# The second layer of a fused scan and maxout kernel as seven half-block products over pairs of 512-token blocks

## The chip, the cores and the metric

One core of a Trainium2 chip runs the whole program. The metric is the device time of one launch in microseconds (us). Each kernel was run several times; the kernel before was run again in the same rounds as every changed kernel. Each run is marked fast or slow: for one core, slow means more than 1.5% above the fastest run of the same kernel. A ratio below is the mean time of one kernel's fast runs over the mean of the other's fast runs of the same rounds, so it is not quite the ratio of the medians that are quoted.

Engines in the profile: PE is the tensor engine (matmuls; PEld its weight loads), DVE the vector engine, ACT the scalar engine, POOL and SP two engines that here do little but start DMA transfers. SPq is SP's instruction queue, in which a transfer that cannot yet be handed over holds up the next. PSUM is the memory that matmuls write their sums to. A transfer has *landed* when its completion is recorded, which can be well after it has left the queue.

## The reference, cut to what matters

```python
# x, f_logit: (4, 6144, 256) float32;  w1, w2: (256, 1024);  w_out: (1024, 256)
f = lower_bound + (1 - lower_bound) * sigmoid(f_logit)
h = 0
for t in range(6144):                     # a gated running sum, per batch and channel
    h = f[:, t] * h + (1 - f[:, t]) * x[:, t]
    y[:, t] = h
y = y.reshape(24576, 256)
out = np.maximum(y @ w1, y @ w2) @ w_out  # float32, (24576, 256)
```

Both kernels use max(a, b) = a + relu(b - a): a first layer relu(y (w2 - w1)), a second layer that multiplies it by w_out, and a linear part y (w1 w_out), whose 256x256 product is made once at the start.

## The kernel before: the parts that matter

The tokens come as 48 blocks of 512. After the first four blocks, input is brought in chunks of 1024 tokens (one chunk is one pair of blocks). For each chunk and each of f_logit and x there are two steps. POOL starts a *fetch*: DRAM to a DRAM scratch buffer, cast from float32 to bfloat16. SP starts a *transpose*: the scratch buffer goes through a transposing DMA into the chip's memory, with channels on partitions. There are two scratch buffers for each input, so the fetch for chunk c+2 waits until the transpose of chunk c has landed.

```python
def fetch(c):                                    # POOL queue
    for s in range(2):                           # f, then x
        scr = scratch[s][uses[s] % NSCR]         # NSCR = 2
        nc.gpsimd.dma_start(out=scr..., in_=srcs[s][b, t0 : t0 + nt, :]...)
        held[c, s] = scr
def cross(c):                                    # SP queue
    for s in range(2):
        dst = inpool.tile([P, KC, CH], BF16, name=("fT", "xT")[s])
        nc.sync.dma_start_transpose(out=dst[:, :, 0:nt], in_=held[c, s][0:nt, :])
# ...
def second_layer(j, slot):                       # block j, an eighth of its matmuls
    # for each 128-token group: 2 linear + 8 matmuls with 128x256 results
    nc.tensor.matmul(ps[:, r, :], lhsT=left, rhs=right, ...)      # L410
    # ... after the last one of two groups
    nc.vector.tensor_copy(out=osb[...], in_=ps[:])                # L430
    if i == ns - 1:
        nc.sync.dma_start(out=out[r0 : r0 + nb, :]..., in_=osb[...])   # store, SP queue
# ...
for j in range(2, NBLK + 1):
    ahead("cross", cross, j + 3)                 # transposes three blocks ahead
    ahead("fetch", fetch, j + 7)                 # fetches seven blocks ahead
    for fc in range(FC):                         # FC = 8
        first_layer(j, fc)                       # two 128x512 matmuls (L381), one relu (L389)
        second_layer(j - 1, fc)                  # ten 128x256 matmuls in two fc's
        # ... gate and scan of block j + 1 between them
```

So SP's queue holds, for each 1024 tokens: transpose f, transpose x, store of one block, store of the next. A store waits until its block is computed, and everything behind it waits with it.

## Time and profile before

| | |
|---|---|
| time, median of the first three runs | 401.07 us (400.53 to 441.09) |
| span of the profiled run | 428.3 us (a slow run) |
| PE work of one pair in an undisturbed stretch | 15.6 us |
| PE / ACT / DVE busy in the profiled run | 92% / 63% / 58% |

The profile is of a slow run: it shows PE waiting in places, where the timed fast runs have almost no room for waits. First, the busy time and the costliest groups. Columns of a group: line, engine, operation, result<-inputs, shapes, count | busy us, mean ns of one | idle us of the engine just before them and what ended most of it. (In all fences, `...` stands for lines left out.)

```profile
PE 392.8 (92%) x2744; PEld 296.8 (69%) x2792; DVE 248.7 (58%) x359; ACT 268.5 (63%) x447; POOL 26.4 (6%) x58
...
L381 PE MATMUL dT<-y,wd 128*128 128x512 bf16 x720 | 219.5, 384 | 21.3 <-ACT rt L389 19.5
L410 PE MATMUL psO<-wob,rt 128*128 128x256 bf16 x1536 | 230.7, 274 | 2.7 <-issue 0.4
```

The next fence is from the waits (engine, line, tile <- what it waited for: us in total, times, longest), and after it one line of the stretch table for 126 to 141.6 us (length; busy us of PE, PEld, DVE, ACT and POOL with their instruction counts; granted PE clock; DMA share; GB/s).

```profile
ACT u L190 <- DMA fT<-scr_1_91: 18.2, 7, 4.6
ACT u L190 <- DMA fT<-scr_0_90: 17.3, 8, 5.2
```

```profile
126.00:141.60 15.60, 15.49 (x112) 11.87 (x113) 10.02 (x14) 10.97 (x19) 0.97 (x2) 1.00 1.25 200
```

The second-layer matmuls and the first-layer ones fill PE: 15.49 of 15.60 us in an undisturbed stretch. ACT waited 35.5 us in all for the transposes of f; that is where this slow run lost its time. The chain that ended last, by engine and by line:

```profile
PE 46%; DMA 34%; SPq 15%; ACT 3%; DVE 1%; issue 1%; ACTq 0%
PE psO L410 25%; DMA fT<-scr_0_90 20%; PE dT L381 19%; SPq L153 13%; DMA fT<-scr_1_91 12%; ACT u L190 2%; DMA w1n_110<-in_moe_w_dram 2%; SPq L433 1%; PE psO L352 1%; ACT rt L389 1%; PE tT L180 1%; PE psO L365 0%; SPq L121 0%; DVE osb L430 0%; DVE y L233 0%
```

Last, the DMA part: the hardware queue's packets (transposes and stores: count, MB, share of 16 engines' span), and the median us from issue to landing of a transpose (the last number).

```profile
q1 hardware_dynamic: 100512, 51.13, 66.7%
...
fT<-scr_0_90 SPq DMA_TRANSPOSE x11, 16.1
xT<-scr_0_92 SPq DMA_TRANSPOSE x11, 9.4
```

### The profile page before, as it was taken

What the parts mean: (1) busy time and instruction counts of PE and PEld (TensorE: products, weight loads), DVE (VectorE), ACT (ScalarE), POOL (GpSimd) and SP (SyncE); (2) the same over time, 40 slices, a digit from 0 to 9 for tenths busy, and PEclk for the clock granted to TensorE, in tenths of its full rate; (3) what the DMA queues carried; (4) which work ended last, traced back from release to release, by engine and by line L of the source; (5) the groups of instructions that cost most, each with busy time, mean ns of one, the idle gap of its engine ahead of it and who ended that gap; (6) DMA issues with size and microseconds to landing.
All of it is one profiled execution on the core that took longest, in us unless ns stands there. A gap on an engine that the chain in (4) does not pass through costs nothing.

```text
span 428.3 us, 6970 instructions
## 1 busy us (share of the span) xinstructions
PE 392.8 (92%) x2744; PEld 296.8 (69%) x2792; DVE 248.7 (58%) x359; ACT 268.5 (63%) x447; POOL 26.4 (6%) x58
## 2 busy tenths in 40 slices
PE   3999979798789999998997899999998999999996
PEld 1677756576557777776775577767676777777775
DVE  5785637455357566564653557657547656567551
ACT  3656656557366676675673666756657676776762
POOL 1400000000000000000000000000000000000000
PEclk9999999999989999999999699999999999999999
DMA  7999999999999999999998999999999999998112
GB/s 245 222 220 198 123 157 141 137 169 252 81 240 226 119 239 233 112 248 168 183 237 75 218 158 186 250 145 170 219 131 231 226 216 164 268 157 179 79 69 100
DMA packets 103377, 77.01 MB, mean 180 GB/s; under 512 B 93552, under 2 KB 94064, under 8 KB 102640
## 3 DMA queue, kind: packets, MB, share of 16 engines
q1 hardware_dynamic: 100512, 51.13, 66.7%
q0 software_dynamic: 2544, 25.17, 36.1%
q8 instruction: 22, 0.36, 0.4%
q10 hardware_dynamic: 288, 0.26, 0.2%
q14 instruction: 11, 0.09, 0.1%
HBM read 53.48 MB, written 48.23 MB: 237 GB/s over the span
## 4 chain that ended last, share of the span: by engine, by line
PE 46%; DMA 34%; SPq 15%; ACT 3%; DVE 1%; issue 1%; ACTq 0%
PE psO L410 25%; DMA fT<-scr_0_90 20%; PE dT L381 19%; SPq L153 13%; DMA fT<-scr_1_91 12%; ACT u L190 2%; DMA w1n_110<-in_moe_w_dram 2%; SPq L433 1%; PE psO L352 1%; ACT rt L389 1%; PE tT L180 1%; PE psO L365 0%; SPq L121 0%; DVE osb L430 0%; DVE y L233 0%
## 5 line engine op out<-in xcount | busy, mean ns | idle before, releaser
L389 ACT ACTIVATE rt<-dT 128x512 bf16<-128x512 f32 x384 | 219.2, 598 | 104.1 <-PE dT L381 100.0
L381 PE MATMUL dT<-y,wd 128*128 128x512 bf16 x720 | 219.5, 384 | 21.3 <-ACT rt L389 19.5
L410 PE MATMUL psO<-wob,rt 128*128 128x256 bf16 x1536 | 230.7, 274 | 2.7 <-issue 0.4
L410 PEld LDWEIGHTS <-rt 128*128 128x128 bf16 x1536 | 170.7, 114 | 41.4 <-issue 1.1
L233 DVE TENSOR_TENSOR_SCAN y<-ff,y,v 128x512 bf16<-128x512 bf16 x88 | 107.9, 1268 | 0.1
L430 DVE COPY osb<-psO 128x512 f32<-128x512 f32 x94 | 64.7, 690 | 59.0 <-PE psO L410 58.9
L381 PEld LDWEIGHTS <-wd 128*128 128x128 bf16 x768 | 75.8, 99 | 33.2 <-issue 24.6
L209 DVE TENSOR_SCALAR ff<-u,nom 128x512 bf16<-128x512 bf16 x94 | 29.0, 351 | 105.0 <-ACT u L190 105.0
L410 PE MATMUL psO<-w_109,y 128*128 128x256 bf16 x384 | 74.0, 275 | 0.0
L410 PEld LDWEIGHTS <-y 128*128 128x128 bf16 x384 | 43.4, 113 | 42.6 <-issue 3.5
L190 ACT ACTIVATE u<-fT 128x1024 bf16<-128x1024 bf16 x44 | 46.4, 1054 | 35.5 <-DMA fT<-scr_1_91 18.2
L220 DVE TENSOR_TENSOR v<-u,xT 128x1024 bf16<-128x1024 bf16 x44 | 30.3, 688 | 3.8 <-DMA xT<-scr_0_92 1.8
L98 POOL DMA_DIRECT2D scr_0_90<-in_f_logit_dram x11 | 5.4, 493 | 149.7 <-DMA fT<-scr_0_90 149.7
L98 POOL DMA_DIRECT2D scr_1_91<-in_f_logit_dram x11 | 5.3, 486 | 148.8 <-DMA fT<-scr_1_91 148.1
L233 DVE TENSOR_TENSOR_SCAN y<-ff,v 128x512 bf16<-128x512 bf16 x6 | 7.0, 1208 | 0.0
L98 POOL DMA_DIRECT2D scr_0_92<-in_x_dram x11 | 5.4, 488 | 18.7 <-DMA xT<-scr_0_92 16.9
L98 POOL DMA_DIRECT2D scr_1_93<-in_x_dram x11 | 5.3, 486 | 15.7 <-DMA xT<-scr_1_93 14.9
L190 ACT ACTIVATE u<-tT 128x1024 bf16<-128x1024 bf16 x3 | 3.2, 1058 | 4.3 <-PE tT L180 4.3
L352 PE MATMUL psO<-ident_f,w1n_110 128*128 128x128 f32 x8 | 1.9, 422 | 3.4 <-DMA w1n_110<-in_moe_w_dram 3.4
L341 ACT ACTIVATE wd<-wdf,om 128x128 bf16<-128x128 f32 (+1 forms) x6 | 2.2, 428 | 4.3 <-DVE wdf L333 4.3
L352 PEld LDWEIGHTS psO<-ident_f,w1n_110 128*128 128x128 f32 x8 | 1.6, 221 | 3.7 <-issue 3.7
L220 DVE TENSOR_TENSOR v<-u,tT 128x1024 bf16<-128x1024 bf16 x3 | 3.6, 1216 | 0.0
(49 smaller groups left out, 45.1 us busy)
## 6 DMA issues: line engine op xcount, KB each, us to landing
out_dram<-osb SPq DMA_DIRECT2D x47, 512.0 KB, 4.8
scr_0_90<-in_f_logit_dram POOLq DMA_DIRECT2D x11, 512.0 KB, 7.5
scr_0_92<-in_x_dram POOLq DMA_DIRECT2D x11, 512.0 KB, 12.4
scr_1_91<-in_f_logit_dram POOLq DMA_DIRECT2D x11, 512.0 KB, 7.9
scr_1_93<-in_x_dram POOLq DMA_DIRECT2D x11, 512.0 KB, 13.6
fn<-in_f_logit_dram POOLq DMA_DIRECT2D x3, 256.0 KB, 7.9
xn<-in_x_dram POOLq DMA_DIRECT2D x3, 256.0 KB, 8.6
w2n_112<-in_moe_w_dram SPq DMA_DIRECT2D x1, 512.0 KB, 6.5
```

What stands on the lines that cost most here:

```text
L98: nc.gpsimd.dma_start(out=scr[0:nt, :].rearrange("(p i) d -> p (i d)", p=P), in_=src.rearrange("(p i) d -> p (i d)", p=P),)
L153: nc.sync.dma_start_transpose(out=dst[:, :, 0:nt], in_=held[c, s][0:nt, :])
L180: nc.tensor.transpose(dst, src, ident[:])
L190: nc.scalar.activation(out=like(u[:, :, 0:nb], fT), in_=fT, func=AF.Sigmoid, scale=-1.0)
L209: nc.vector.tensor_scalar(out=ff[:, h, 0:nb], in0=u[:, h, 0:nb], scalar1=nom[:, h : h + 1], scalar2=1.0, op0=ALU.mult, op1=ALU.add,)
L220: nc.vector.tensor_tensor(out=like(v[:, :, 0:nb], xT), in0=like(u[:, :, 0:nb], xT), in1=xT, op=ALU.mult,)
L233: nc.vector.tensor_tensor_scan(out=y[:, h, 0:nb], data0=ff[:, h, 0:nb], data1=v[:, h, 0:nb], initial=init, op0=ALU.mult, op1=ALU.add,)
L352: nc.tensor.transpose(pt[:, kc, q, :], half(w1n, g)[:, kc, 2 * r + q], ident_f[:])
L381: nc.tensor.matmul(dT[:, 0:nb], lhsT=wd[:, kc, fc * P : (fc + 1) * P], rhs=y[:, kc, 0:nb], start=(kc == 0), stop=(kc == KC - 1),)
L389: nc.scalar.activation(out=rt[:, 0:nb], in_=dT[:, 0:nb], func=AF.Relu)
L410: nc.tensor.matmul(ps[:, r, :], lhsT=left, rhs=right, start=(s == 0 and (r == 0 or j == NBLK - 1)), stop=(s == n - 1 and (r == 1 or j == N ...
L430: nc.vector.tensor_copy(out=osb[:, 2 * g : 2 * g + 2, :], in_=ps[:])
```

## The change

The intent is to do less PE work. The second layer multiplies relu(...) of two blocks by w_out, split into halves: a 2x2 by 2x2 block product. Strassen's method (in Winograd's form) needs seven half products in place of eight. For a pair, 64 + 16 matmuls of 128x256 become seven products of 16 and four linear parts of 8, all 128x128. In exchange there are four bfloat16 sums of 128x2048 on DVE, three float32 sums out of PSUM on DVE, three snapshots and a copy on ACT. The relu now takes two PSUM banks in one instruction and writes its result in the permuted order which makes the second layer's weight loads contiguous. The work is now scheduled by pairs, and with it the input: f and x are transposed and fetched with different leads, and the first of the two stores of a pair is ready later in the pair than before (after matmul 120 of the 144).

```diff
-    inpool = ctx.enter_context(tc.tile_pool(name="inp", bufs=5))
+    inpool = ctx.enter_context(tc.tile_pool(name="inp", bufs=4))
-    def fetch(c):
+    def fetch(c, s):
-    def cross(c):
+    def cross(c, s):
# ... first layer: one relu of two chains, permuted result
-        nc.scalar.activation(out=rt[:, 0:nb], in_=dT[:, 0:nb], func=AF.Relu)
+        if fc % 2:
+            nc.scalar.activation(
+                out=rts[j, k][:, g - 1 : g + 1, :].rearrange("p q (i m) -> p q i m", m=P),
+                in_=dT[:].rearrange("p q (m i) -> p q i m", m=P),
+                func=AF.Relu,
+            )
# ... second layer of a pair (ja, jb), 144 matmuls
+        product("X", part(0, 0), lambda k: wob[:, k, lo], True)
+        then(snapshot("X", 1))
+        product("B", part(0, 1), lambda k: wob[:, KH + k, lo], True)
+        linear("B", ja, lo, False)
+        then(leave("B", ja, lo, 1, False))
+        product("X", sub(2), lambda k: t2[:, k, :])
+        then(snapshot("X", 2))
+        product("E", sub(1), lambda k: t1[:, k, :], True)
+        then(snapshot("E", 5))
+        product("X", sub(3), lambda k: t3[:, k, :])
+        linear("X", jb, hi, False)
+        then(leave("X", jb, hi, 5, False))
+        product("E", sub(4), lambda k: wob[:, KH + k, hi])
+        linear("E", ja, hi, False)
+        then(leave("E", ja, hi, 2, True))         # store of ja
+        product("X", part(1, 1), lambda k: t4[:, k, :])
+        linear("X", jb, lo, True)
+        then(leave("X", jb, lo, None, True))      # store of jb
# ... start: f one chunk further than x
-        ahead("cross", cross, 4)
+        for s in range(2):
+            ahead("cross", cross, s, 5 - s)
+        ahead("fetch", fetch, 1, 5)
+        ahead("fetch", fetch, 0, 6)
# ... main loop
-        for j in range(2, NBLK + 1):
-            ahead("cross", cross, j + LEAD_CROSS)
-            ahead("fetch", fetch, j + LEAD_FETCH)
+        for p in range(PAIR0, NPAIR):
+            for s in range(2):
+                ahead("cross", cross, s, chunk_of(p + 3) - s)   # f(p+3), x(p+2)
+            for s in range(2):
+                ahead("fetch", fetch, s, chunk_of(p + 5) - s)   # f(p+5), x(p+4)
```

## The prediction

> **What bounds the kernel now.** The tensor engine (PE). By groups, the first layer's 128x512 matmuls (L381) and the second layer's 128x256 matmuls (L410) run back to back: in the timeline eight 128x256 ones take 0.88 us and sixteen slots repeat every 7.82 us per 512-token block when nothing stalls (stretch table: 15.49 of 15.60 us PE busy, granted clock 1.00). That is 216 ns per 128x512 and 109 ns per 128x256. All 1920 L410, 768 L381 and the small matmuls sum to about 385 us; with some 11 us before the first weights and 4 us at the end that is 400, the timed 401.07. The profiled execution (428.3 us) is about 20 us longer because PE waits in several stretches behind late fT transposes (waits: ACT u <- fT 35 us; DMA busy 99%). The timed runs leave almost no room for such stalls. DVE is 58% busy, ACT 63%.
>
> **Removed.** Per pair of blocks (1024 tokens) 80 matmuls of 128x256 (8.74 us of PE); four 0.69 us DVE copies of results; 16 relus of 0.60 us (about 0.51 back to back).
>
> **Added, per pair.** PE: seven products of 16 plus four linear parts of 8: 144 matmuls of 128x128. The transposes of the trace are 128x128 matmuls, each with its own weight load, at eight per 0.445 us, 55.6 ns: 8.0 us. So PE goes from 15.64 to 14.94 us per pair, -0.70 us, for 21 pairs: -14.7 us. Halving the width gives back about 0.2 us of the arithmetic saving of 0.85 us.
> DVE: four bf16 sums of 2048 elements. The drive product (1024 elements, 688 ns) gives an estimate of 1.22 us each, as "VectorE: DVE Perf Modes" in the Trainium skill (perf-mode tier table) has it for this size. Three f32 adds out of PSUM, about 0.70 each; decay in two ops of about 0.45. With the scans (4.9) and drives (1.4): about 14.1 us of 14.94, 94%, against 10.6 of 15.6 before.
> ACT: eight relus of 128x1024 (about 1.0 us; the gates that read PSUM with a stride, 1.02 us, show no price for it), four gates of 0.60, four copies of 0.58: about 12 of 14.94. Not a limit, if nothing queues behind a late gate.
> DMA: same bytes, 4.7% less time for them; transposes are issued about a chunk earlier, which should remove some waits.
>
> **Critical path.** All of the PE saving lies on it as long as DVE keeps up (slack under 1 us per pair) and transposes arrive every 14.94 us. Ideal: 386 us. I add 4 us for the weight loads of y that still step by four tokens (113 ns against 98 contiguous; unproven at 55.6 ns pitch; 32 per pair), for DVE lateness at PSUM hand-over, and for DMA.
>
> **Predicted: 390 us, range 383 to 400. Faster by over 2%: 0.58; within 2%: 0.36; slower by over 2%: 0.06.**
>
> **What would show each step.** PE: 128x128 matmuls near 55.6 ns pitch and a pair near 14.9 us in undisturbed stretches. If y's strided loads do not hide, the linear parts' pitch is above 60 ns. DVE: 90-95% busy in such stretches, sums 1.22 us, leaves 0.70. ACT: relu about 1.0 us, no stride price. Waits: no large PE wait on DVE sums or leaves; fT waits fewer than before.
>
> **What would make it wrong.** (1) Strided weight loads at 128 columns cost 15 ns or more each: 0.5 us per pair, two thirds of the gain. (2) DVE ops longer than estimated, making DVE the period (15.5 us or more). (3) Transposes unable to come every 14.9 us, so that the saving becomes waits on fT or xT. (4) Relus on two banks at once leaving first-layer matmuls waiting on ACT.

## The result and the profile after

The changed kernel is correct, and slower: a median of 449.91 us (441.9 to 462.32, 5 runs) against 400.93 us (400.53 to 441.09, 5 runs). The ratio of fast runs is 1.111, 95% interval 1.099 to 1.122. The profile is of the 462.32 us run, which counts as slow among the kernel's own runs; no run of this kernel came within 10% of a fast run of before, and the profile of a variant whose run counted as fast (x lead, below) shows the same picture.

Busy time and groups first, to be set against those of before:

```profile
PE 386.3 (84%) x4064; PEld 286.1 (62%) x4136; DVE 322.4 (70%) x383; ACT 290.8 (63%) x383; POOL 26.5 (6%) x58
...
L426 ACT ACTIVATE r<-dT 128x1024 bf16<-128x1024 f32 x192 | 196.3, 1025 | 115.9 <-PE dT L418 115.1
...
L596 PE MATMUL ps<-t,S 128*128 128x128 bf16 x1008 | 85.7, 230 | 50.1 <-DVE S L487 49.7
...
L596 PEld LDWEIGHTS <-y 128*128 128x128 bf16 x672 | 49.6, 113 | 16.4
L554 DVE TENSOR_TENSOR osb<-ps,sn 128x512 f32<-128x512 f32 x63 | 42.8, 679 | 13.2 <-PE ps L596 7.6
...
L487 DVE TENSOR_TENSOR S<-r 128x2048 bf16<-128x2048 bf16 x42 | 51.1, 1217 | 0.0
```

A stretch without a wait (same columns as before), and one run of PE in the timeline (start, length, what):

```profile
380.00:396.00 16.00, 15.84 (x188) 11.92 (x188) 14.71 (x17) 12.85 (x18) 0.49 (x1) 1.00 1.04 193
```

```profile
84.97 0.61 PE L596 MATMUL ps<-w13d,y 128*128 128x128 bf16 x8
```

The engines did what was planned. In the chain between 382.5 and 392 us, every slot of nine 128x128 and two 128x512 matmuls takes 0.93 us, 14.9 us for 16 slots of a pair. Eight matmuls with y's strided weight loads end 0.61 us after the start of the first; take off the mean of one (219 ns) and seven spacings are left of 56 ns each: the stride does not show. Sums take 1217 ns, adds 679 ns, relus 1025 ns.

The loss is in waits:

```profile
POOL scr L100 <- DMA fT<-scr: 306.2, 20, 35.0
...
DVE v L205 <- DMA xT<-scr: 77.7, 18, 23.3
...
PE ps L596 <- DVE S L487: 49.7, 14, 22.2
...
ACT u L267 <- DMA fT<-scr: 29.9, 4, 18.4
```

```profile
PE 33%; SPq 28%; DMA 23%; issue 3%; ACT 3%; DVE 1%; POOL 0%; ACTq 0%; POOLq 0%
SPq L149 27%; PE ps L596 17%; PE dT L418 13%; DMA xT<-scr 10%; DMA scr<-in_x_dram 7%; DMA fT<-scr 6%; PE ps L465 2%; DVE S L487 1%; ACT r L426 1%; SPq L437 1%; ACT u L267 1%; ACT osb L552 1%; ACT sn L542 0%; POOL scr L100 0%; DVE osb L474 0%
```

PE's 49.7 us on DVE's sums is not DVE being slow: the sums stand behind the drive product v, which waited 77.7 us for transposes of x. In the chain, the tensor engine has fallen from 46% to 33%, and the line that issues the transposes (L149) alone holds 27%. The timeline of SP's queue and of POOL shows a steady bad state:

```profile
229.67 8.29 SPq L149 DMA_TRANSPOSE fT<-scr  x1
238.05 9.46 SPq L149 DMA_TRANSPOSE xT<-scr  x1
247.61 1.01 SPq L437 DMA_DIRECT2D out_dram<-osb  x2
248.71 9.82 SPq L149 DMA_TRANSPOSE fT<-scr  x1
```

```profile
229.91 0.49 POOL L100 DMA_DIRECT2D scr<-in_f_logit_dram  x1 [15.35 <-DMA fT<-scr]
231.24 0.49 POOL L100 DMA_DIRECT2D scr<-in_x_dram  x1 [0.85 <-DMA xT<-scr]
248.40 0.49 POOL L100 DMA_DIRECT2D scr<-in_f_logit_dram  x1 [16.67 <-DMA fT<-scr]
251.62 0.49 POOL L100 DMA_DIRECT2D scr<-in_x_dram  x1 [2.73 <-DMA xT<-scr]
```

SP is never idle: a transpose of f (8.29 us in the queue), one of x (9.46), two stores (1.01), and at once the next f. From f to f it is 19.0 us, where PE needs 14.95. POOL's f fetch waits until the transpose of f has landed (248.40), which is 18.7 us after it began and just before the next one starts; the x fetch follows 1.3 us later in one of the laps shown and 3.2 us later in the other. So both fetches run beside transposes.

There is also one hole. The chain around it (start, length, what), and a stretch in it:

```profile
73.63 33.96 DMA scr<-in_x_dram
...
107.64 4.40 DMA xT<-scr
```

```profile
96.70:100.70 4.00, 0.00 (x0) 0.00 (x0) 0.00 (x0) 0.00 (x0) 0.00 (x0) 0.50 0.79 10
```

POOL had issued three fetches within 2 us (73.15, 73.63 and 75.10), beside a transpose of f; PE stands still in this stretch, with 10 GB/s moved, and on to 108 us. The lap with the hole (from one transpose of f to the next) lasts 38.5 us, 24 more than PE needs; the sixteen laps after it lose 40 us together. The hole comes back in the profiles of e1, e12 and e16 below (laps of 39.2, 48.6 and 38.6 us), but not in those of e11 and e20 (longest lap 25.8 and 23.9 us), which are as slow: it adds to the loss, and the loss does not need it. Why that one fetch took 34 us is not shown. The DMA part:

```profile
q1 hardware_dynamic: 100512, 51.13, 67.8%
...
fT<-scr SPq DMA_TRANSPOSE x22, 16.5
xT<-scr SPq DMA_TRANSPOSE x22, 9.3
```

The same packets and bytes as before, and transposes that land 16.5 and 9.3 us after issue, against 16.1 and 9.4 in the slow profile of before. The queue's share of 67.8% is of a longer span: 312 us of each DMA engine against 286 in the slow profile of before.

### The profile page after: what moved, and what is told of

It is laid out like the page before. It is cut to its first block, busy times and chain, and to the rows that moved or that the text cites. A ratio compares the mean times of both kernels' runs of the same rounds, so it can differ in the third digit from the quotient of the medians.

```text
span 460.2 us, 9454 instructions
## 1 busy us (share of the span) xinstructions
PE 386.3 (84%) x4064; PEld 286.1 (62%) x4136; DVE 322.4 (70%) x383; ACT 290.8 (63%) x383; POOL 26.5 (6%) x58
## 3 DMA queue, kind: packets, MB, share of 16 engines
q1 hardware_dynamic: 100512, 51.13, 67.8%
## 4 chain that ended last, share of the span: by engine, by line
PE 33%; SPq 28%; DMA 23%; issue 3%; ACT 3%; DVE 1%; POOL 0%; ACTq 0%; POOLq 0%
SPq L149 27%; PE ps L596 17%; PE dT L418 13%; DMA xT<-scr 10%; DMA scr<-in_x_dram 7%; DMA fT<-scr 6%; PE ps L465 2%; DVE S L487 1%; ACT r L426 1%; SPq L437 1%; ACT u L267 1%; ACT osb L552 1%; ACT sn L542 0%; POOL scr L100 0%; DVE osb L474 0%
## 5 line engine op out<-in xcount | busy, mean ns | idle before, releaser
L426 ACT ACTIVATE r<-dT 128x1024 bf16<-128x1024 f32 x192 | 196.3, 1025 | 115.9 <-PE dT L418 115.1
L596 PEld LDWEIGHTS <-S 128*128 128x128 bf16 x1344 | 94.9, 103 | 91.4 <-DVE S L487 52.0
L596 PE MATMUL ps<-t,S 128*128 128x128 bf16 x1008 | 85.7, 230 | 50.1 <-DVE S L487 49.7
L205 DVE TENSOR_TENSOR v<-u,xT 128x1024 bf16<-128x1024 bf16 x44 | 30.3, 688 | 77.7 <-DMA xT<-scr 77.7
L596 PEld LDWEIGHTS <-r 128*128 128x128 bf16 x1008 | 66.9, 98 | 27.3
L418 PEld LDWEIGHTS <-wd 128*128 128x128 bf16 x768 | 62.7, 100 | 19.6 <-issue 11.6
L267 ACT ACTIVATE u<-fT 128x512 bf16<-128x512 bf16 x88 | 54.9, 627 | 30.0 <-DMA fT<-scr 29.9
L554 DVE TENSOR_TENSOR osb<-ps,sn 128x512 f32<-128x512 f32 x63 | 42.8, 679 | 13.2 <-PE ps L596 7.6
L596 PE MATMUL ps<-wob,r 128*128 128x128 bf16 x672 | 51.2, 219 | 0.5
L487 DVE TENSOR_TENSOR S<-r,S 128x2048 bf16<-128x2048 bf16 x42 | 50.8, 1210 | 0.9 <-ACT r L426 0.9
L487 DVE TENSOR_TENSOR S<-r 128x2048 bf16<-128x2048 bf16 x42 | 51.1, 1217 | 0.0
L596 PE MATMUL ps<-w,y 128*128 128x128 bf16 x504 | 48.7, 219 | 0.4
L195 DVE TENSOR_SCALAR ff<-u,nom 128x1024 bf16<-128x1024 bf16 (+2 forms) x54 | 23.9, 454 | 28.6 <-ACT u L267 24.3
L465 PEld LDWEIGHTS <-r 128*128 128x128 bf16 x192 | 19.0, 99 | 4.1 <-issue 0.6
```

The lines of the kernel that those rows point to most:

```text
L195: nc.vector.tensor_scalar(out=ff[:, h, cols], in0=u[:, h, cols], scalar1=nom[:, h : h + 1], scalar2=1.0, op0=ALU.mult, op1=ALU.add,)
L205: nc.vector.tensor_tensor(out=like(v[:, :, cols], xT), in0=like(u[:, :, cols], xT), in1=xT, op=ALU.mult,)
L267: nc.scalar.activation(out=mids[p + NBLK, "u"][:, h, cols], in_=held[c, 0][:, h, cols], func=AF.Sigmoid, scale=-1.0,)
L418: nc.tensor.matmul(dT[:, fc % 2, :], lhsT=wd[:, kc, fc * P : (fc + 1) * P], rhs=y[:, kc, :], start=(kc == 0), stop=(kc == KC - 1),)
L426: nc.scalar.activation(out=rts[j, k][:, g - 1 : g + 1, :].rearrange("p q (i m) -> p q i m", m=P), in_=dT[:].rearrange("p q (m i) -> p q i ...
L465: nc.tensor.matmul(ps[:, r, :], lhsT=left, rhs=right, start=(s == 0 and (r == 0 or j == NBLK - 1)), stop=(s == n - 1 and (r == 1 or j == N ...
```

## The experiments

Expectations name theories by letters: A, the short period leaves DMA too little time; C, the fetches' 32768-byte packets hold up the transposes' 256-byte packets; D, x is transposed too late; E, fetches run beside transposes; H, the late place of the stores; H2, H together with a crowded start. Where another letter appears, the text beside it says what is meant. For each run three readings from the trace are used below: the *lap* (from one transpose of f to the next in SP's queue, one per pair), the mean time of the f and x transposes in SP's queue between 130 and 360 us, and the *first f fetch*, in us after the start of the lap's f transpose.

| kernel | runs, us | f, x transposes in SP's queue, us | 256-byte packets, mean ns |
|---|---|---|---|
| before, slow profile | span 428.3 | 8.1, 7.4 | 35.2 |
| before, null edit, fast profile | 400.45, 400.9, 401.45; slow 430.58 | 2.9, 2.6 | 23.4 |
| after | 442 to 462 | 9.1, 7.3 | 40.0 |
| before, 14.98 us period | 384.8 to 385.4 | 3.4, 2.4 | 23.4 |
| after, x lead (profiled run fast) | 431 to 446 | 8.9, 7.5 | 34.9 |
| after, fetch order exchanged | 398.0 to 402.1 | 7.1, 4.0 | 26.4 |
| after, no fetches from chunk 8 | 392.4 to 399.5 | 3.0, 2.4 | 23.2 |

The kernel before thus has both states too: its slow executions (410 to 441 us, 12 of the 53 runs) show, in the one that was profiled, the same long transposes as the changed kernel.

### Is the period too short? (e1, e2)

e1 lengthens the changed kernel's pair to 15.6 us with zero matmuls. e2 shortens the period of before to 14.98 us by leaving out six of 80 matmuls (the result is wrong).

```diff
# e1, in linear(), changed kernel: 12 more matmuls per pair, adding zero
+            for i in range(3):
+                steps.append([b, ops[0][0], zero[:], i, None, False, None])
# e2, in second_layer(), kernel before
+            if s == 4 and i < 3:
+                continue
```

> The changed kernel with 12 matmuls of 128x128 on a zero tile added per pair (result unchanged), so that a pair of blocks takes PE 15.6 us as before the change instead of 14.9. Theory A (the DMA engines keep up with a period of 15.6 us but not with 14.9, and once behind they run at 18 us per chunk): the run comes near the kernel before, 400 to 410 us, and no PE wait on S sums. Theory B (what the change did to the order and lead of its own transposes, x one chunk later than f, makes them late whatever the period): stays at 435 to 460 us.

> The kernel before with 6 of 80 second-layer matmuls left out per pair (wrong result on purpose), so that its period is 14.98 us, with its own order of DMAs. Theory A: it falls behind too and is slower than before, 425 to 460 us. Theory B: PE bound, 400.9 less 23 x 0.66 = 386 us.

e1: 463.41, 458.7, 447.36, 451.23 us, ratio 1.121 (1.112 to 1.130). e2: 385.05, 384.8, 385.43, 385.1 us, ratio 0.961. In e1's profiled run six laps in a row take 15.6 us (from 126 to 219 us), and then most take 17 to 22, so the lengthened kernel reached its period and lost it again. Theory A falls twice: giving back before's period does not help the changed kernel, and before's order of transfers keeps a 14.98 us period without a single slow run. e2 also says what this chip does at that period when nothing waits: 385 us, so the 386 us of the prediction's PE sum was sound. Its queue:

```profile
249.37 3.37 SPq L153 DMA_TRANSPOSE fT<-scr  x1
252.83 3.28 SPq L153 DMA_TRANSPOSE xT<-scr  x1
256.43 7.83 SPq L435 DMA_DIRECT2D out_dram<-osb  x2
264.36 2.90 SPq L153 DMA_TRANSPOSE fT<-scr  x1
```

```profile
257.15 0.49 POOL L98 DMA_DIRECT2D scr<-in_f_logit_dram  x1 [12.73 <-DMA fT<-scr]
258.75 0.49 POOL L98 DMA_DIRECT2D scr<-in_x_dram  x1 [1.11 <-DMA xT<-scr]
```

The transposes leave the queue in 3.4 and 3.3 us; then the two stores hold SP for 7.8 us. The f fetch is started at 7.8 us of the lap, when the transpose of f has landed, and the x fetch at 9.4, when that of x has. The packets of the two fetches run from 9.6 us of this lap on and no transpose packet starts beside them.

### Are the packets too large? (e3, e4)

Each fetch is split into four DMAs of 256 rows, which makes packets of 8192 bytes in place of 32768; e3 in the changed kernel, e4 in before.

```diff
+            for q in range(4):
+                rows = slice(q * nt // 4, (q + 1) * nt // 4)
                 nc.gpsimd.dma_start(out=scr[rows, :]..., in_=src[rows, :]...)
```

> The changed kernel with each 1024-token fetch issued as four DMAs of 256 rows, so its packets are 8 KB instead of 32 KB. Theory C (a refinement of A: while a 32 KB fetch packet of 2.5 us runs on an engine, the transpose's 256-byte packets wait behind it, one per fetch packet, so transposes crawl during every fetch): transposes land in well under 16 us and the time falls to 386 to 400 us. If the DMA engines are simply out of throughput, or the leads are wrong: no change, 440 to 460 us.

> The kernel before with the same split. Theory C: 400 us as before, as it is bound by PE when fast, but with transposes landing sooner and without the slow executions of 441 us. Throughput theory: as before, or slower for the extra issues.

e3: 477.14, 447.94, 437.99, 457.85 us. e4: 405.06, 422.21, 474.3, 420.32 us. No help: e3's one fast run of 438 us lies 4 us below the changed kernel's best, and of e4's four runs three are slow (before: 2 of 7 in the same rounds). With one fast run each there is no ratio. The packet records say why. Time of the 256-byte transpose packets, summed and divided by 16 engines, by how long one took:

```
                      under 0.1 us   0.1 to 0.5    0.5 to 1      over 1 us
before (null edit)    105.4          6.8           3.4 (76)      16.2 (152 packets)
after                 103.5          7.2           5.8 (128)    108.9 (938 packets)
e3, 8192-byte fetch   101.8         20.9          89.1 (2245)    30.0 (315 packets)
order exchanged (e6)  103.2          5.9           7.1 (156)     32.8 (336 packets)
```

All that the transposes lose in the changed kernel, 93 us of every DMA engine, is in some 900 packets of 90112, which took 1.8 us in the median, of the order of one fetch packet (a 32768-byte one takes 2.45 us in the median). With packets a quarter as long there are more and shorter waits (those over 0.5 us take 0.64 us in the median, a fetch packet 0.62), and the sum is no smaller. The Trainium skill says that each DMA engine takes turns between its queue rows packet by packet ("DMA: Bandwidth & Descriptors", section "Queues, rings and completion order"); these records agree: the wait scales with the other queue's packet, and cutting it only multiplies the turns. Theory C fits a single wait and is wrong as a remedy.

### Is it the lead of x, the fetches, or their order? (e5, e6, e10)

e5 gives x the same lead as f. e6 exchanges the two fetches in the main loop and nothing else. e10 leaves out all fetches from chunk 8 on (old data in the scratch, wrong).

```diff
# e5: one of five changed lines
-                ahead("cross", cross, s, chunk_of(p + 3) - s)
+                ahead("cross", cross, s, chunk_of(p + 3))
# e6: the loop around the fetches
-            for s in range(2):
+            for s in (1, 0):
                 ahead("fetch", fetch, s, chunk_of(p + 5) - s)
# e10: in fetch()
+            held[c, s] = scr
+            if c >= 8:
+                return
```

> The changed kernel with x transposed and fetched as far ahead as f (both for pair p+3 and p+5; before, x was one pair nearer). Theory D (x's lead of one pair, behind f in the queue, is what holds PE): the wait of the DVE drive on xT goes, and the time falls to 386 to 395 us. Theory E (fetches run at the same time as transposes and make them slow, a state that holds itself, whatever the lead): PE still waits, then on both, 430 to 460 us.

> The changed kernel with only the order of the two fetches on the POOL queue exchanged: x first. As x's fetch waits until xT, the second transpose, has landed, both fetches then start after both transposes, instead of f's fetch running beside xT. Theory E: the transposes get short (under 10 us to landing), 386 to 400 us. Theory D: no change, 440 to 460 us.

> The changed kernel without the fetches from chunk 8 on; the transposes read old scratch (wrong result on purpose). If fetches beside transposes are the cause (Theory E): transposes land in under 7 us and the time is 386 to 390 us, which is also the PE bound of the change. If transposes and stores alone are too much or the lead alone is too short: over 400 us.

e5: 436.84, 446.44, 431.48, 434.14 us, ratio 1.078: 14 us better than the changed kernel by the medians, still far off, and the waits move to f (46.9 us of ACT). Theory D is a side matter. e10: 392.61, 395.72, 399.53, 392.4 us, ratio 0.981 (386 to 390 was expected; f transposes landed after 5.9 us in the median, as expected). e6: 397.97, 400.85, 402.14, 400.3 us, ratio 0.9975 (0.991 to 1.004): a one-line change takes back about 50 us. That is at the upper end of the expected 386 to 400 us, and f transposes landed after 11.6 us in the median, not under 10. Waits in e6, and the stretch from 175 to 375 us in e6, in e10 and in after, in this order:

```profile
DVE v L205 <- DMA xT<-scr: 12.7, 5, 6.3
...
ACT u L267 <- DMA fT<-scr: 7.7, 2, 5.3
```

```profile
175.00:375.00 200.00, 197.74 (x2314) 150.00 (x2354) 176.71 (x198) 158.29 (x211) 10.24 (x21) 1.00 0.88 188
```

```profile
175.00:375.00 200.00, 197.74 (x2313) 150.06 (x2355) 173.28 (x194) 158.04 (x210) 0.00 (x0) 1.00 0.52 129
```

```profile
175.00:375.00 200.00, 172.77 (x1891) 128.77 (x1924) 146.94 (x165) 133.20 (x176) 10.74 (x22) 0.94 1.15 174
```

Waits on transposes are down from 107.6 us to 20.4, and e6's PE is as busy in that stretch as with no fetches at all: 197.74 of 200 us, against 172.77. Over these 200 us the changed kernel is behind e6 by 423 matmuls, some 37 us at e6's rate: 25 us of it is idle time of PE, the rest longer matmuls (91 us busy for 1000 of them against 85) at a granted clock of 0.94. The clock seems to follow the waits and not to make them: it is 1.00 in the quiet stretch above and 0.50 where PE stands still. So the steady loss goes when the fetches go (e10), and their order is enough to decide it (e6). Before fetches f first as well and is fast in most runs, so it is the order within the changed schedule that matters. The trace does not fully say why. A lap of e6, in SP's queue and in POOL's:

```profile
235.39 6.54 SPq L149 DMA_TRANSPOSE fT<-scr  x1
242.02 5.30 SPq L149 DMA_TRANSPOSE xT<-scr  x1
```

```profile
235.33 0.75 POOL L100 DMA_DIRECT2D scr<-in_x_dram  x1 [15.07 <-DMA xT<-scr]
236.08 0.49 POOL L100 DMA_DIRECT2D scr<-in_f_logit_dram  x1
```

In e6 POOL's queue stands at the x fetch until the transpose of x has landed, so the two fetches go out together, once both transposes of a lap have landed: in most laps that is at its end or within the first 3 us of the next. The x transpose is through the queue in 4.0 us in place of 7.3. But the f transpose of the next lap still runs beside the fetches (7.1 us). The two transposes together stay below 14.95 us, so SP still comes to a wait for a store. The packet records show what differs. Taken together, the packets of a lap's two fetches are on the DMA engines for 11.5 us in the changed kernel (10.0 to 13.5 us, 11 laps between 130 and 330 us), and 715 to 1723 of the 4096 transpose packets of a pair start among them. In e6 it is 6.5 us (5.1 to 8.0, 13 laps) with 0 to 975 packets, and in e2 7.1 us with none. So in e6, where the two go out together, they are sooner out of the way, and fewer packets of the transposes get between theirs.

### A null result (e8)

e8 was meant to make before issue both stores together at the end of a lap.

> The kernel before with the two stores of a pair issued together at the end of the pair, as the changed kernel has them, instead of one in the middle and one at the end. Theory F (two stores at the end of a period, in front of the next transposes, push the kernel into the slow state): 430 to 460 us. Otherwise 401 us.

It held back the first store's issue in program order, but SP's queue still had the stores in the same order with the same waits for data (8.15 us on the two, issued in the same places). 400.45, 400.9, 430.58, 401.45 us, ratio 0.999. The edit did not do what it was for, so this tests nothing. Its use is a fast profile of before's schedule.

### Is it the start? (e11, e12, e13, e14)

e11 has three scratch buffers, which should spread the fetches of the start. e12 holds PE for some 15 us once, at the fourth pair, so that the input can get ahead. e13 is e6 with three scratch buffers and x's first transpose ahead of the second of f. e14 holds back before's fetches from the fifth chunk on until the scan of block 1, which crowds its start.

```diff
# e11 and e13
-    NSCR = 2
+    NSCR = 3
# e12, changed kernel
+            if p == PAIR0 + 3:
+                idle = ps_d.tile([P, 2, TB], FP32, name="dT")
+                for _ in range(270):
+                    nc.tensor.matmul(idle[:, 0, 0:P], lhsT=ident[:], rhs=zero[:], start=True, stop=True)
# e13, besides e6's line and NSCR
-        for s in range(2):
-            ahead("cross", cross, s, 5 - s)
+        for s, c in ((0, 4), (1, 4), (0, 5)):
+            ahead("cross", cross, s, c)
# e14, kernel before
-        ahead("fetch", fetch, 4)
+        ahead("fetch", fetch, 3)
# ... after recurrence(1)
+        pool_waits(ys[1][:, 1, TB - 1 : TB])
+        ahead("fetch", fetch, 4)
```

> The changed kernel with three scratch buffers per input instead of two, so that a fetch no longer waits for the transpose two chunks earlier but three, and the third chunk is fetched at the start. If the late fill at the start is what puts the changed kernel into the slow state: 386 to 405 us. If the overlap of fetches and transposes in the steady part does it whatever the start: 430 to 460 us.

> The changed kernel with 270 matmuls on a zero tile (15 us of PE, once, result unchanged) at the start of the fourth pair, so that the DMAs catch up once. Theory G (two states, and only the start decides: once a fetch begins about 7 us after the period's first transpose, it ends before the next one and the state holds): one delay of 15 us and then periods of 14.9 us, 400 to 415 us in all, shorter than without the delay. If the changed kernel has no such lasting state: it falls back within some periods, 445 us or more.

> x's fetch first (as e6) with three scratch buffers and the first x transpose moved in front of the second f transpose. e6 ran in periods of 14.95 us from 75 us on and lost about 7 us between 30 and 75 us to late transposes. If those were the late fill: 388 to 394 us, faster than the kernel before by 2 to 3%.

> The kernel before with the fetches of its fifth and later chunks held until block 1's scan is done (about 26 us instead of 14), so that its DMAs start late. Theory G: it starts in the slow state and stays there, 420 to 450 us. If the kernel before always finds back: the delay alone, 405 to 412 us.

e11: 460.81, 407.14, 461.87, 448.72 us. e12: 458.84, 415.72, 408.34, 439.27 us. e13: 412.45, 400.5, 408.98, 405.61, 401.95, 401.15 us, no better than e6. e14: 439.03, 407.38, 407.48, 406.86 us, ratio of fast runs 1.016. Single runs of e11 and e12 at 407 and 408 us suggest that the changed kernel has a fast state as well, and e12's profile shows it being entered and lost. The first f fetch of each lap, us after the lap's start, from the delay on, and the same reading of e2 from its third lap on:

```
e12:  5.5  7.3  6.1  8.6 10.9 11.0 11.4 12.0 12.2 13.1 21.2 17.0 18.4
e2:  11.5 11.4 11.4  9.9  9.0  8.2  7.1  7.8  6.1  6.5  7.0  6.5  7.3
```

Before's schedule starts out of place and drifts inward; the changed kernel's drifts outward until, after ten laps, the fetches meet the next transposes and laps grow from 14.9 to between 16 and 21 us. The profile of the changed kernel itself has the end of such a drift: after the hole its laps take 15.1 and 14.9 us with the first f fetch at 12.7 and 14.2 us, then it comes at 15.7 and 18.1 us and the laps take 16 to 19. e14 agrees: before, put out of place at its start, found back in three runs of four at a cost of 6 us.

### Does the place of the stores make the drift? (e15, e16)

In before's schedule the two stores go out about 7 and 14.5 us into a lap. In the changed kernel running without waits they go out at 12.0 and 14.5 (read from e6 and e10), since both blocks of a pair are finished late. e15 puts both stores of e2 at the end of the lap, this time with the later one first in the queue so that the edit takes effect. e16 is e12 with the first store of a pair queued behind the next pair's transposes.

```diff
# e15, on e2 (wrong on purpose)
+                    kept.insert(0, (r0, nb, osb))
+                    if j % 2 or j == NBLK - 2:
+                        for r, m, o_ in kept:
                             nc.sync.dma_start(out=out[r : r + m, :]..., in_=o_[:, 0:ns, :])
+                        kept.clear()
# e16, on e12
-                if last:
+                if last and j % 2 == 0 and p < NPAIR - 2:
+                    late.append((j, osbs[j]))
+                elif last:
                     store(j, osbs[j])
# ... in the main loop, behind the transposes
+            while late:
+                store(*late.pop())
```

> The before kernel with a second layer shortened to a 14.98 us pair period (the earlier run: 385 us, stores at 7.1 and 14.6 us of the period), now with the stores of both blocks of a pair queued together at the end of the period. Theory H (the changed kernel falls into the slow state because both of its stores come late in the period and run into the x fetch and the next f transpose): the periods grow beyond 15 us and the time goes above 400 us. Rival (the place of the stores does not matter): 384 to 388 us with periods of 15.0. The result is wrong on purpose, as in the earlier run.

> The changed kernel with the 15 us delay at its start (earlier: 459, 416, 408, 439 us; its fast state drifts and breaks after about ten periods), and the first of the two stores of each pair queued behind the next pair's transposes, about 5 us into the period instead of at 12 us. Theory H: the drift of the first f fetch within the period stops (stays below 11 us of 15), the fast state holds to the end and the times lie close together at 402 to 412 us. Rival: the times scatter from 408 to 460 us as before.

e15: 408.31, 393.56, 398.02 and 384.56 us, where e2 had four runs within 0.7 us. In three runs of four, moving the stores alone took away the steadiness of that schedule. In its profiled run the first f fetch does not come inward (12 to 14 us for a dozen laps) and then breaks out:

```profile
190.01 9.89 SPq L153 DMA_TRANSPOSE fT<-scr  x1
...
204.09 0.81 SPq L439 DMA_DIRECT2D out_dram<-osb  x2
```

The f transpose takes 9.9 us in the queue (e2: 3.4). e16: 438.01, 451.71, 403.86, 456.53, 453.04, 408.89 us. The profiled run (438.01) lost all its time before 156 us; from then on the first f fetch stays at 8.7 to 10.6 us and every lap is 14.9 or 15.0 us, 14 laps to the end:

```profile
155.87 4.70 SPq L149 DMA_TRANSPOSE fT<-scr  x1
160.66 3.00 SPq L149 DMA_TRANSPOSE xT<-scr  x1
163.75 6.97 SPq L438 DMA_DIRECT2D out_dram<-osb  x2
170.81 5.95 SPq L149 DMA_TRANSPOSE fT<-scr  x1
```

So where it was reached, the fast state held in the run that was looked at, with the stores holding SP for 5 to 7 us (7.8 in e2). But the expected times did not come: four runs of six stayed slow, so a moved store does not bring the kernel out of the slow state, nor does the delay always.

### Can a version beat both kernels? (e17, e18, e19, e20)

e17 is e5 and e6 together. e18 is e6 with the first transposes and fetches in the order of need. e19 is e18 with e16's moved store. e20 is the changed kernel with e18's start and the moved store, but its own order of fetches.

```diff
# e18, e19, e20: start (first place, then second)
-        for s in range(2):
-            ahead("cross", cross, s, 5 - s)
-        ahead("fetch", fetch, 1, 5)
-        ahead("fetch", fetch, 0, 6)
+        for s, c in ((0, 4), (1, 4), (0, 5)):
+            ahead("cross", cross, s, c)
+        for s, c in ((1, 5), (0, 6), (1, 6)):
+            ahead("fetch", fetch, s, c)
# ...
-        for s in range(2):
-            ahead("cross", cross, s, 6 - s)
-            ahead("fetch", fetch, s, 7 - s)
+        for s, c in ((1, 5), (0, 6)):
+            ahead("cross", cross, s, c)
+        for s, c in ((0, 7), (1, 7), (0, 8)):
+            ahead("fetch", fetch, s, c)
```

> The changed kernel with x transposed as far ahead as f (alone: 431 to 446 us) and the two fetches of a period exchanged (alone: 398 to 402 us). If the loss that is left with the exchange alone comes from x arriving too late in the first periods (30 to 75 us), this gives 388 to 396 us. If it is the burst of fetches at the start whatever the lead, 398 to 402 us. If the exchange works only because x is fetched one period after f's place in the order, so that the longer lead brings the overlap back, over 415 us.

> The changed kernel with the two fetches of a period exchanged (alone: 398 to 402 us, with some 7 to 10 us lost between 30 and 75 us), and with the first transposes and fetches of the start in the order in which their data is needed (x of the first 1024-token chunk before f of the second), spread over three places instead of three fetches at one. If the order at the start is what still costs: 390 to 396 us and PE busy over 9.5 of every 10 us from 30 to 80 us. If not: 398 to 402 us.

> The same with the first store of each pair moved behind the next pair's transposes. If the store's place matters only where f is fetched first (the exchange has already taken the fetches out of the transposes' way): the same as e18_order_start to 1 %. If it still matters: 2 to 5 us less, and fewer slow runs.

> The changed kernel with its own fetch order (f first), the mended start and the moved store, without the delay. Theory H2 (the crowded start sends the kernel into the slow state, the late store keeps the fast state from lasting; the f-first order by itself is harmless, as it is in the kernel before): 390 to 402 us in most runs, the first f fetch at 5 to 11 us of each period. Rival (the fetch order itself is needed): most runs 420 us and over.

| | runs, us | ratio of fast runs |
|---|---|---|
| e17 | 399.65, 406.51, 401.25, 420.07, 402.34, 402.22 | 1.0015 (0.999 to 1.004) |
| e18 | 428.62, 407.1, 427.88, 411.37, 412.68, 405.38 | 1.017 (1.012 to 1.023) |
| e19 | 404.59, 418.89, 412.25, 402.11, 403.0, 441.26 | 1.0055 (1.003 to 1.008) |
| e20 | 453.8, 444.04, 439.56, 439.93, 451.43, 419.44 | one fast run alone |

No version beats before. All four miss the better times hoped for. e18's order of need was worse than e6's start: its profiled run has 14.9 us laps and then one lap of 36.7 us. e19 against e18 is in favour of the moved store, but both scatter. e20 speaks against H2: with this start and the store moved, the f-first order still runs slow in every run but one, and that one is at 419 us. Its laps in the trace are 14.1 to 24 us from the fifth on. What the order of need did to the start was not good either (a lap of 23.9 us at 79 us), so e20 does not show that a clean start would not help; it shows that this one does not.

## Why the prediction was wrong, point by point

- *What bounds the kernel.* Right. PE at 15.6 us per pair; e2's 385 us for 14.98 us shows that the fast runs follow PE's period.
- *PE: 14.94 us per pair.* Right to the last digit that can be read: 14.9 in the chain, laps of 14.9 and 15.0 in e6, e10 and e16.
- *y's strided weight loads.* Feared, and not there: 113 ns each (98 contiguous), but 56 ns from matmul to matmul. The Trainium skill ("TensorE: Matmul & The Clock Gate", section "Weight-path perf modes — Fast Weight Load (FWL) and DoubleRow") lists the fast read pattern as packed or strided, which agrees with the spacing.
- *DVE.* Right. Sums 1217 ns; the table in "VectorE: DVE Perf Modes", section "The perf-mode tier table (the rule you actually need)", has 1224 ns for this operation and size. Adds 679 ns against 0.70 us, and DVE is busy 14.71 of 16.00 us in the quiet stretch, 92%.
- *ACT.* Right: relus 1025 ns, no price for the stride, 12.85 of 16.00 us.
- *DMA.* Wrong, and this is the step that failed, as it was put: "same bytes, 4.7% less time for them; transposes are issued about a chunk earlier, which should remove some waits", with 4 us for weight loads, DVE lateness and DMA together. The bytes are the same, but not the time that they take: the transposes' packets took 40.0 ns in the mean against 23.4 in a fast run of before's schedule, because the fetches and the transposes of the changed schedule run into each other in nearly every lap. Waits on f transposes were a little fewer, as said (29.9 us against 35.5 in before's slow profile), but those on x transposes went from 3.5 us to 77.7, 107.6 us in all, and the kernel's time to 450 us.
- *"Transposes unable to come every 14.9 us"* stood under what would make the prediction wrong, and that is what the profile shows. But it was thought of as a matter of the period, and e1 and e2 show that the period is not it.

The sum, from the fast runs: without fetches (e10) 393.6 us in the mean, so about 56 of the 450 us go when the fetches go. (That takes away the waits for their data as well as their traffic beside the transposes.) e6, which keeps every fetch, gives back about 50 of these. Of e10's 393.6, some 7 to 8 us above the 386 of PE's sum are lost at the start, where PE is busy 7.7 to 8.2 of 10 us in two stretches (30 to 40 and 60 to 70 us); e17 to e19 did not get them back.

What is shown: the loss goes with the fetches (e10), and as e6 moves them only, it is their place beside the transposes and not the traffic as such; the order of two fetches is enough to decide it (e6); late stores were enough to make before's steady order unsteady in three runs of four (e15). What is supported by one profile only: that an earlier store keeps the changed kernel's fast state (e16). What stays open: why the changed kernel with f first hardly reaches the fast state, or loses it, whatever was done to its start (e1, e11, e12, e20); why two fetches that go out together let fewer transpose packets between theirs, which is measured in e6 but not explained; and the one fetch of 34 us.

## What to carry to other kernels

Cutting PE's work also moves every transfer that is tied to it, so cost the transfers again as a timetable of one period: when each fetch, transpose and store starts, what releases it, and what else is on the DMA engines at that moment. Look for slack in the queue: here the one that the stores held for 7.8 us of each lap found back from a bad start (e2), the one with 2.8 us drifted and was lost (e12), and one that never waits is itself the period (laps of 19 us in the changed kernel). When a kernel that should be faster is slower and its engines' durations are all as planned, exchange the order of two DMA issues before redesigning anything: here one line was worth 50 us, though it brought the kernel back to the time of before and not below it.

## What the Trainium skill lacked or had wrong

- "DMA: Bandwidth & Descriptors", section "Rules for kernel authors", says that a transpose next to ordinary DMAs needs nothing. That held for the results, which were correct in every variant meant to be; it lacks the price. Beside fetches (DRAM to DRAM with a cast, started by POOL) the median f transpose landed after 16.5 us, and after 6.7 us in e2, where they are apart.
- The same page, "Queues, rings and completion order", has the turn-taking by packet, but not what it does to small packets: 938 of 90112 transpose packets of 256 bytes made 108.9 of their 225 us per DMA engine, and cutting the fetch packets from 32768 to 8192 bytes did not lower the sum (242 us in e3).
- "TensorE: Matmul & The Clock Gate", section "Back-to-back issue gap", gives about 81 ns per matmul of 128 columns in a real kernel with a weight load each. Here it was 56 ns in streams of 128x128 matmuls between 128x512 ones, with weight loads of 98 to 113 ns beside them; the section has 56 ns only as the gap without a budget for weight loads.
- No page speaks of two lasting states of one program that differ, as far as these traces show, in how its DMA queues stand to each other: 401 or 410 to 441 us for before, 404 to 457 us for e16.
